# Fetching K and V of a decode-attention kernel in 4 MB transfers of 32 KB runs, eight heads interleaved, instead of 1 MB transfers of 8 KB runs

## The chip, the cores and the metric

The kernel runs on one core of one Trainium2 chip. The metric is the time of one execution on the device in microseconds (us). A run is in a *slow* state when it lies over 1.5% above the fastest of the same kernel; a single run of a kernel has the state *unknown*.

## The reference

One decode step: four batches, one new token each, attention over the last 2,048 of 8,192 cached positions, added to a small MLP.

```python
# x (4,1,576); k_cache, v_cache (4,16,8192,128) bf16; wq (576,4096); wo (4096,576)
xn = layernorm(x)
q  = (xn @ wq) -> (4, 32 heads, 1, 128)
k  = k_cache[:, :, 8192-2048:, :]         # each of 16 heads serves two q heads
v  = v_cache[:, :, 8192-2048:, :]
p  = softmax(q k^T * 128**-0.5)           # (4,32,1,2048)
attention = (p v) @ wo
mlp = x1 + gelu(layernorm(x1) @ w3) @ w4  # x1 = xn + gelu(layernorm(xn) @ w1), shifted, @ w2
out = x + attention + mlp
```

K and V in the window are 4 x 16 x 2048 x 128 x 2 bytes each, 67.1 MB together. The profile counts 88.5 MB read in all.

## The kernel before

Every transfer of K, V and the weights comes from one queue, in the order in which the program lists it. K comes into a ring of 7 slots and V into a ring of 9, each slot 1 MB. One unit of K or V is one head of two batches. Its source is written as 64 outer rows, each with 2 runs of 8 KB; together they fill 128 partitions.

```python
NKU, NVU, NT = 7, 9, 32
UE = NT * 128                               # 4096 bf16 = 8 KB in each partition

def kv_pairs(ring_t, slot, cache, u):
    g, pr = u // 2, u % 2
    return [(ring_t[:, slot * UE:(slot + 1) * UE],
             cache[pr:B:2, g, Sk - W:Sk, :].rearrange("b (i t) d -> i b (t d)", t=NT))]   # i 64, b 2

for u in range(NU):                         # NU = 32 units of K ...
    ev_k.append(add_dma(kv_pairs(kring_t, u % NKU, A_k_cache, u), ("k", u % NKU),
                        [f"T{4 * (u - NKU) + 3}"] if u >= NKU else [], u))
for u in range(NU):                         # ... then 32 of V, wo, w1, w2 among them
    ...
    ev_v.append(add_dma(kv_pairs(vring_t, u % NVU, A_v_cache, u), ("v", u % NVU), w, kk))
```

TensorE turns each 128x128 piece of K (`T{n}`), VectorE and ScalarE copy the turned piece out (`E{n}`), and products with a padded q give the scores (`SC`). After the last K, ScalarE takes the exponential, 32 transposes turn P, and products of V with P follow V as it lands. At the end w3 comes, then w4 in five pieces, whose 72 products (36 rows of 128, two halves of the columns) finish the sum:

```python
AO_CH = ((0, 4), (4, 7), (7, 8))            # the products with wo, in three pieces
W4P = [(0, 3, 0), (3, 6, 2), (6, 8, 4)]     # w4: pieces of 12, 12, 8, then 3 and 1 rows of 128
...
if n < last_p:
    add("pe", f, waits=[ev_w4[n], "gelu2"], sig=f"MO{n}", key=KT + 20 + n)
```

Of the kernel before, what the change touches and what calls it, by code (L numbers as in the profile page):

```python
# [12 lines left out]
NKU = 7  # L13
NVU = 9
# [5 lines left out]
WO_AFTER = 9  # L20
W12_AFTER = 11
AO_CH = ((0, 4), (4, 7), (7, 8))
# [13 lines left out]

def bass_parallel_sum__sliding_block_cached__mixer_s_mlp__decode_kernel(
# [8 lines left out]
    G = Hkv  # L46
    NU = 2 * G
    NT = 32
    UE = NT * 128
    NHB = 4 * NU  # L50
# [4 lines left out]
    HCH = [(0, 128), (128, 128), (288, 128), (416, 128), (256, 32), (544, 32)]  # L55
    x2 = A_x.rearrange("b s d -> (b s) d")
    o2 = out.rearrange("b s d -> (b s) d")

    with ExitStack() as ctx:
# [5 lines left out]

        kring_t = sb("kring", [128, NKU * UE], BF16)
        vring_t = sb("vring", [128, NVU * UE], BF16)
        W3E = 4 * F + FH
        regB_t = sb("regB", [128, max(NKT * 1024, W3E)], BF16)
        kring = kring_t[:].rearrange("p (s t d) -> p s t d", s=NKU, t=NT)  # L70
        vring = vring_t[:].rearrange("p (s t d) -> p s t d", s=NVU, t=NT)
        ktbuf = regB_t[:, 0:NKT * 1024].rearrange("p (s t d) -> p s t d", s=NKT, t=8)
        w3main = regB_t[:, 0:4 * F].rearrange("p (r n) -> p r n", r=4)
        w3rag = regB_t[:, 4 * F:W3E]
        wqmain = vring_t[:, 0:4 * Hq * Dh].rearrange("p (r n) -> p r n", r=4)
        wqrag = vring_t[:, 4 * Hq * Dh:4 * Hq * Dh + Hq * Dh // 2]
        WQ_SLOTS = -(-(4 * Hq * Dh + Hq * Dh // 2) // UE)
        wo_sb = kring_t[:, 0:Hq * D].rearrange("p (h r n) -> p h r n", h=8, r=4)
        _o = Hq * D
        w1main = kring_t[:, _o:_o + 4 * D].rearrange("p (r n) -> p r n", r=4)  # L80
        _o += 4 * D
        w1rag = kring_t[:, _o:_o + HALF]
        _o += HALF
        w2main = kring_t[:, _o:_o + 4 * D].rearrange("p (r n) -> p r n", r=4)
        _o += 4 * D
        w2rag = kring_t[:, _o:_o + HALF]
        _o += HALF
        assert _o <= NKU * UE
# [17 lines left out]
        Qpad_t = sb("Qpad", [128, 130 * G], BF16)  # L106
        Qpad = Qpad_t[:, 0:128 * G].rearrange("p (g b c) -> p g b c", g=G, b=B)
        ident_bf = sb("ident_bf", [128, 128], BF16)
        ident_f = sb("ident_f", [128, 128], FP32)
        ones_f = sb("ones_f", [128, 128], FP32)  # L110
        diag = sb("diag", [128, 128], FP32)
# [7 lines left out]
        P_sb = sb("P_sb", [128, NT, 64, 2], BF16)  # L119
        PT = sb("PT", [128, NT, 128], BF16)  # L120
# [3 lines left out]
        out_sb = sb("out_sb", [B, D], BF16)  # L124
# [4 lines left out]
        PTps = [ps[:, 4 + k, :].bitcast(BF16).rearrange("p (t r) -> p t r", t=8) for k in range(4)]  # L129
# [3 lines left out]
        OTbank = {g: 6 - n for n, (a, z) in enumerate(AO_CH) for g in range(2 * a, 2 * z)}  # L133
        OTps = lambda g: ps[:, OTbank[g], 0:128]
# [28 lines left out]
        def rag_src(w_ap):  # L163
            return w_ap[512:576, :].rearrange("r (h n) -> (r h) n", h=2)

        KS = float(NHB + 4)
        KV = KS + 4.0
        KT = KV + NU + 8.0


        P = lambda *a, **k: add("pool", *a, **k)
        P(lambda e: e.memset(zeros_bf[:], 0.0), sig="zeros_bf", key=-100)
        P(lambda e: e.memset(ident_bf[:], 1.0), sig="ib1", key=-99)
        P(lambda e: e.affine_select(out=ident_bf[:], in_=ident_bf[:], compare_op=ALU.is_equal, fill=0.0, base=0,
                                    pattern=[[-1, 128]], channel_multiplier=1), waits=["ib1"], sig="ident_bf", key=-98)
        P(lambda e: e.memset(ragsrc[:], 0.0), sig="rag_zero", key=-97)
        P(lambda e: e.memset(Qpad_t[:], 0.0), sig="qpad_zero", key=-96)
        P(lambda e: e.memset(P_sb[:], 0.0), sig="p_zero", key=-95)
        P(lambda e: e.memset(ident_f[:], 1.0), sig="if1", key=-94)
        P(lambda e: e.affine_select(out=ident_f[:], in_=ident_f[:], compare_op=ALU.is_equal, fill=0.0, base=0,  # L180
                                    pattern=[[-1, 128]], channel_multiplier=1), waits=["if1"], sig="ident_f", key=-93)
# [3 lines left out]

        ev_x = add_dma([(x_sb[:], x2)], "x", (), -100, engine="act")
        ev_wq, ev_k, ev_v, ev_w4 = [], [], [], []
        wq_src = A_wq[0:512, :].rearrange("(p r) n -> p r n", r=4)
        for r in range(4):
            ev_wq.append(add_dma([(wqmain[:, r, :], wq_src[:, r, :])], ("wq", r), (), -20 + r))  # L190
        ev_wq.append(add_dma([(wqrag, rag_src(A_wq))], ("wq", 4), (), -15))

        def kv_pairs(ring_t, slot, cache, u):
            g, pr = u // 2, u % 2
            return [(ring_t[:, slot * UE:(slot + 1) * UE],
                     cache[pr:B:2, g, Sk - W:Sk, :].rearrange("b (i t) d -> i b (t d)", t=NT))]

        def last_unit(nslots, s_lo, s_hi):
            return max(u for u in range(NU) if s_lo <= u % nslots <= s_hi)

        for u in range(NU):
            ev_k.append(add_dma(kv_pairs(kring_t, u % NKU, A_k_cache, u), ("k", u % NKU),
                                [f"T{4 * (u - NKU) + 3}"] if u >= NKU else [], u))
        wo_wait = f"T{4 * last_unit(NKU, 0, (_o - 1) // UE) + 3}"
        for u in range(NU):
            kk = KS + 0.01 * u
            w = [f"PV{u - NVU}"] if u >= NVU else (["q"] if u < WQ_SLOTS else [])
            ev_v.append(add_dma(kv_pairs(vring_t, u % NVU, A_v_cache, u), ("v", u % NVU), w, kk))
            if u == WO_AFTER - 1:
                wo_d = wo_sb.rearrange("p h r n -> p h (r n)")  # L210
                wo_s = A_wo.rearrange("(h p r) n -> p h (r n)", h=8, r=4)
                wo_8 = A_wo.rearrange("(h a p r) n -> h a p (r n)", h=8, a=8, r=4)
                ev_wo = add_dma([(wo_d[:, 0:6, :], wo_s[:, 0:6, :])] + [(wo_d[:, h, :], wo_8[h]) for h in (6, 7)],
                                "wo", [wo_wait], kk + 0.005)
            if u == W12_AFTER - 1:
                ev_w1 = add_dma([(w1main, B_w1[0:512, :].rearrange("(p r) n -> p r n", r=4)), (w1rag, rag_src(B_w1))], "w1",
                                [wo_wait], kk + 0.005)
                ev_w2 = add_dma([(w2main, B_w2[0:512, :].rearrange("(p r) n -> p r n", r=4)), (w2rag, rag_src(B_w2))], "w2",
                                [wo_wait], kk + 0.006)
        w3_src = B_w3[0:512, :].rearrange("(p r) n -> p r n", r=4)  # L220
        ev_w3 = [add_dma([(w3main[:, r, :], w3_src[:, r, :])], ("w3", r), [f"SC{G - 1}"], KT + r) for r in range(4)]
        ev_w3.append(add_dma([(w3rag, rag_src(B_w3))], ("w3", 4), [f"SC{G - 1}"], KT + 4))
        w4_main = B_w4[0:4096, :].rearrange("(c p r) n -> p c (r n)", p=128, r=4)
        w4_t3 = B_w4[4096:4480, :].rearrange("(p r) n -> p (r n)", r=3)
        w4_t1 = B_w4[4480:4608, :]
        w4tile = {}
        ev_w4 = []
        s4 = (NU - NVU) % NVU
        assert all((s4 + s_) % NVU + 2 <= NVU for s_ in (0, 2, 4))
        W4P = [(0, 3, 0), (3, 6, 2), (6, 8, 4)]  # L230
        for n, (c0, c1, s_) in enumerate(W4P):
            o0 = (s4 + s_) % NVU * UE
            v = vring_t[:, o0:o0 + (c1 - c0) * 4 * D].rearrange("p (c rn) -> p c rn", c=c1 - c0)
            ev_w4.append(add_dma([(v, w4_main[:, c0:c1, :])], ("w4", n), [f"PV{NU - NVU + s_ + 1}"], KT + 5 + n))
            for c in range(c0, c1):
                for q in range(4):
                    w4tile[4 * c + q] = v[:, c - c0, q * D:(q + 1) * D]
        o0 = (s4 + 4) % NVU * UE + 2 * 4 * D
        assert 2 * 4 * D + 4 * D <= 2 * UE
        v3 = vring_t[:, o0:o0 + 3 * D]  # L240
        v1 = vring_t[:, o0 + 3 * D:o0 + 4 * D]
        wl = [f"PV{NU - NVU + 5}"]
        ev_w4.append(add_dma([(v3, w4_t3)], ("w4", 3), wl, KT + 8))
        ev_w4.append(add_dma([(v1, w4_t1)], ("w4", 4), wl, KT + 9))
        for q in range(3):
            w4tile[32 + q] = v3[:, q * D:(q + 1) * D]
        w4tile[35] = v1
        W4N = [(12 * n, 12 * n + 12) for n in range(2)] + [(24, 32), (32, 35), (35, 36)]
        ev_o = [None, None]
        for h, eng in ((0, "sp"), (1, "act")):  # L250
            ev_o[h] = add_dma([(o2[:, HALF * h:HALF * (h + 1)], out_sb[:, HALF * h:HALF * (h + 1)])], ("out", h),
                              [f"fin{h}"], 10000, engine=eng)
            add(eng, lambda e: None, [ev_o[h]], None, 10001)
# [47 lines left out]
        for r in range(5):  # L301
            add("pe", pe_q(r), waits=[ev_wq[r], "xnT"], sig="q" if r == 4 else f"q_{r}", key=-30 + r)
# [310 lines left out]
```

## Time and profile before

| | before |
|---|---|
| time, median of 3 runs | 224.78 us (224.45 to 224.97) |
| span of the profiled run | 223.5 us |
| bytes read | 88.5 MB, of them K and V 67.1 MB |
| rate in 60 to 160 us | 418 GB/s |
| packet of 8,192 bytes | 312 ns (median of the packet records) |
| busiest engine | TensorE, 73% |

The first view is the page's span cut into 40 equal slices, of the kernel before. TensorE's and DMA's rows are busy tenths, PEclk is the clock granted to TensorE in tenths, GB/s is what the DMA engines moved.

```profile
PE   0469999999999999997257731666974436977596
...
PEclk9999999999999999999855555555695555875579
DMA  6999999999999999999999999999999999999940
GB/s 250 424 421 421 418 422 421 418 425 416 416 424 418 418 424 419 422 416 419 419 417 407 415 411 418 419 422 419 419 419 418 421 419 421 422 413 408 411 177 1
```

From the second to the 38th slice the DMA row stands at 9 and the rate at 407 to 425 GB/s. TensorE is nearly full as well up to the 18th slice, where K is turned, but the DMA row has no gap there, so its queue is not held up. Later TensorE has time to spare. The DMA bounds this kernel: 88.5 MB at 418 GB/s is 212 us of a span of 223.5.

The stretches of the end, of the kernel before (the window and its length, each engine's busy us with the instruction count in brackets, then granted clock, DMA share, GB/s; PE is TensorE, PEld its weight loads, DVE VectorE, ACT ScalarE, POOL GpSimd):

```profile
core 0: us, PE busy (x) PEld busy (x) DVE busy (x) ACT busy (x) POOL busy (x), PEclk, DMA share, GB/s
...
204.00:208.00 4.00, 2.59 (x70) 2.39 (x67) 0.00 (x0) 0.29 (x1) 0.00 (x0) 0.50 1.02 408
208.00:212.00 4.00, 2.59 (x11) 1.36 (x12) 0.00 (x0) 0.00 (x0) 0.00 (x0) 0.50 1.02 412
212.00:216.00 4.00, 4.00 (x21) 2.23 (x20) 0.00 (x0) 0.00 (x0) 0.00 (x0) 0.58 0.60 236
216.00:220.00 4.00, 4.00 (x35) 2.80 (x33) 0.00 (x0) 0.00 (x0) 0.00 (x0) 1.00 0.12 45
220.00:223.50 3.50, 1.30 (x11) 0.68 (x8) 0.45 (x1) 0.40 (x1) 0.00 (x0) 1.00 0.01 1
```

From 212 us the DMA is only partly busy, yet TensorE still works to 221. The next two lines are groups of the page for the kernel before: line, engine, operation, tiles, shapes and count; then busy us and the mean ns of one; then the idle time just before them and its releaser.

```profile
L324 PE MATMUL ps<-ident_bf,kring 128*128 128x128 bf16 x1024 | 67.2, 222 | 0.4 <-ACT regB L330 0.2
...
L426 PE MATMUL ps<-vring,h2T_sb 128*4 128x288 bf16 x72 | 11.9, 340 | 2.7 <-DMA vring<-in_B_w_dram 2.7
```

K's transposes (L324) have only 0.4 us of idle time before them: K is always there when TensorE is ready. The timeline has w4's 72 products begin at 209.41 us, when w4's first piece lands, and take 11.89 us.

### The profile page before, as it was taken

How to read it: one execution, taken by the hardware profiler on the slowest of the kernel's cores; microseconds unless marked ns; L12 is line 12 of the kernel's file. 1: busy time of each engine (PE TensorE's matmuls, PEld its weight loads, DVE VectorE, ACT ScalarE, POOL GpSimd, SP SyncE). 2: the span in 40 equal slices, each digit the busy share in tenths (PEclk: the TensorE clock that was granted, in tenths of full speed). 3: DMA queues.
4: the chain of work that ended last, by engine and by line, in shares of the span. 5: the costliest groups of instructions: out<-in, count | busy, mean ns of one | idle time of the engine just before them, and what ended most of it. 6: DMA issues, size and time to landing. Idle time of an engine off the chain costs nothing.

```text
span 223.5 us, 6245 instructions
## 1 busy us (share of the span) xinstructions
PE 162.7 (73%) x2934; PEld 124.7 (56%) x2934; DVE 70.9 (32%) x124; ACT 62.1 (28%) x76; POOL 7.9 (4%) x14
## 2 busy tenths in 40 slices
PE   0469999999999999997257731666974436977596
PEld 0457777777777777775047631544564335666263
DVE  5803565666666556664440000051000000000000
ACT  2001555555555555555594000001100000000000
POOL 8500000000000000000000000000000000000000
PEclk9999999999999999999855555555695555875579
DMA  6999999999999999999999999999999999999940
GB/s 250 424 421 421 418 422 421 418 425 416 416 424 418 418 424 419 422 416 419 419 417 407 415 411 418 419 422 419 419 419 418 421 419 421 422 413 408 411 177 1
DMA packets 13714, 88.91 MB, mean 398 GB/s; under 512 B 1388, under 2 KB 1784, under 8 KB 4472
## 3 DMA queue, kind: packets, MB, share of 16 engines
q1 hardware_dynamic: 13672, 88.50, 95.9%
q8 instruction: 23, 0.38, 0.7%
q14 instruction: 3, 0.02, 0.0%
q10 hardware_dynamic: 16, 0.01, 0.0%
HBM read 88.49 MB, written 0.00 MB: 396 GB/s over the span
## 4 chain that ended last, share of the span: by engine, by line
PE 47%; DMA 34%; ACT 12%; SPq 2%; issue 2%; DVE 1%
PE ps L324 23%; DMA vring<-in_A_v_cache_dram 15%; DMA vring<-in_B_w_dram 14%; PE ps L426 9%; ACT regB L330 8%; PE ps L340 8%; DMA vring<-in_A_wq_dram 5%; PE ps L405 5%; ACT P_sb L366 3%; SPq L159 2%; PE ps L312 1%; DVE rmax L360 1%; PE ps L375 0%; ACT PT L382 0%; PE ps L297 0%
## 5 line engine op out<-in xcount | busy, mean ns | idle before, releaser
L324 PE MATMUL ps<-ident_bf,kring 128*128 128x128 bf16 x1024 | 67.2, 222 | 0.4 <-ACT regB L330 0.2
L324 PEld LDWEIGHTS ps<-ident_bf,kring 128*128 128x128 bf16 x1024 | 58.5, 99 | 13.9 <-issue 7.3
L331 DVE COPY regB<-ps 128x1024 bf16<-128x1024 bf16 x80 | 52.3, 687 | 36.4 <-PE ps L324 34.6
L330 ACT ACTIVATE regB<-ps 128x1024 bf16<-128x1024 bf16 x48 | 47.5, 1022 | 48.4 <-PE ps L324 48.4
L405 PE MATMUL ps<-PT,vring 128*128 128x4 bf16 x1024 | 30.8, 166 | 29.9 <-DMA vring<-in_A_v_cache_dram 27.1
L405 PEld LDWEIGHTS ps<-PT,vring 128*128 128x128 bf16 x1024 | 29.0, 103 | 34.0 <-DMA vring<-in_A_v_cache_dram 28.8
L340 PE MATMUL ps<-regB,Qpad 128*32 128x512 bf16 x256 | 17.5, 392 | 4.5 <-ACT regB L330 4.5
L516 ACT ACTIVATE h2T_sb<-ps 128x144 bf16<-128x144 f32 x1 | 0.3, 291 | 49.6 <-PE ps L510 49.6
L426 PE MATMUL ps<-vring,h2T_sb 128*4 128x288 bf16 x72 | 11.9, 340 | 2.7 <-DMA vring<-in_B_w_dram 2.7
L440 DVE TENSOR_TENSOR OTn<-ps,rinvB 128x64 bf16<-128x64 f32 (+2 forms) x3 | 0.6, 202 | 38.5 <-PE ps L405 38.5
L340 PEld LDWEIGHTS ps<-regB,Qpad 128*32 128x32 bf16 x256 | 5.3, 94 | 11.1 <-ACT regB L330 5.9
L426 PE MATMUL ps<-kring,ORT 128*4 128x288 bf16 x64 | 11.0, 342 | 0.3 <-DVE ORT L444 0.3
L426 PEld LDWEIGHTS ps<-vring,h2T_sb 128*4 128x4 bf16 x72 | 7.1, 99 | 7.3 <-DMA vring<-in_B_w_dram 2.8
L262 ACT ACTIVATE sd<-mv 4x1 f32<-4x1 f32 x3 | 0.6, 202 | 35.0 <-DVE mv L260 35.0
L375 PE MATMUL ps<-ident_bf,P_sb 128*128 128x128 bf16 x32 | 4.1, 308 | 6.6 <-ACT P_sb L366 6.6
L531 DVE CAST out_sb<-ps 4x288 bf16<-4x288 f32 x1 | 0.4, 446 | 25.7 <-PE ps L426 25.7
L426 PEld LDWEIGHTS ps<-kring,ORT 128*4 128x4 bf16 x64 | 6.1, 99 | 4.4 <-DVE ORT L444 0.4
L478 DVE TENSOR_TENSOR x_bf<-ps,xn_bf 4x288 bf16<-4x288 f32 x2 | 0.9, 446 | 23.5 <-PE ps L473 23.5
L501 PE MATMUL ps<-x1nT,regB 128*128 128x4 bf16 x144 | 5.3, 172 | 3.0 <-DMA regB<-in_B_w_dram 2.9
L375 PEld LDWEIGHTS ps<-ident_bf,P_sb 128*128 128x128 bf16 x32 | 3.1, 138 | 7.9 <-ACT P_sb L366 7.9
L366 ACT ACTIVATE P_sb<-ps,negb 64x512 bf16<-64x512 f32 x8 | 6.6, 826 | 2.6 <-DVE negb L361 2.5
L276 PE MATMUL ps<-ident_bf,xn_bf 4*128 4x4 bf16 x8 | 0.5, 166 | 8.8 <-DVE ragsrc L269 8.4
(78 smaller groups left out, 69.7 us busy)
## 6 DMA issues: line engine op xcount, KB each, us to landing
kring<-in_A_k_cache_dram SPq DMA_DIRECT2D x32, 1024.0 KB, 12.1
vring<-in_A_v_cache_dram SPq DMA_DIRECT2D x32, 1024.0 KB, 21.2
regB<-in_B_w_dram SPq DMA_DIRECT2D x4, 1152.0 KB, 26.4
vring<-in_A_wq_dram SPq DMA_DIRECT2D x4, 1024.0 KB, 7.8
kring<-in_A_wo_dram SPq DMA_DIRECT2D x1, 3456.0 KB, 21.1
vring<-in_B_w_dram SPq DMA_DIRECT2D x2, 1728.0 KB, 30.9
kring<-in_A_wo_dram SPq DMA_DIRECT2D x2, 576.0 KB, 21.4
kring<-in_B_w_dram SPq DMA_DIRECT2D x2, 576.0 KB, 13.4
```

What stands on the lines that cost most here:

```text
L159: e.dma_start(o_, i_).then_inc(S[skey], 16)
L312: ins = e.matmul(ps[:, 4 + (w % NTB), :], lhsT=zeros_bf[:, 0:128], rhs=zeros_bf[:, :], start=True, stop=True)
L324: ins = e.transpose(tb[n % NTB][:, t, :], kring[:, u % NKU, 8 * k + t, :], ident_bf[:])
L330: return "act", lambda e: e.activation(out=ktbuf[:, n % NKT], in_=tb[n % NTB], func=ACTF.Copy)
L331: return "dve", lambda e: e.tensor_copy(out=ktbuf[:, n % NKT], in_=tb[n % NTB])
L340: ins = e.matmul(Sps[32 * b:32 * b + 32, c4, :].rearrange("p (t i) -> p t i", t=8), lhsT=Qpad[:, g, b, :], rhs=ktbuf[:, n % NKT, :, bh:128:2],
L360: add("dve", lambda e: e.tensor_reduce(out=rmax[:], in_=Sps, axis=AX.XY, op=ALU.max), waits=[f"SC{G - 1}"], sig="rmax", key=KS)
L366: add("act", lambda e, q=q, s=s, bh=bh: e.activation(out=P_sb[s, 8 * q:8 * q + 8, :, bh], in_=Sps[s, q, :].rearrange("p (t i) -> p t i", t ...
L375: ins = e.transpose(PTps[q][:, t, :], P_sb[:, 8 * q + t, :, :].rearrange("p i b -> p (i b)"), ident_bf[:])
L405: ins = e.matmul(o_, lhsT=vring[:, u % NVU, t, :], rhs=r_, start=(t == 0), stop=(t == NT - 1))
L426: return e.matmul(ACC[h], lhsT=lhsT, rhs=rhs, start=start, stop=stop)
L501: ins = e.matmul(H2Tps[:, n, :], lhsT=w3main[:, r, lo:hi:st], rhs=x1nT[:, r, :], start=(r == 0 and n == 0), stop=False, skip_group_check=True)
```

## The change

The intent is longer runs: 32 KB in each packet instead of 8 KB, so that fewer packets carry their fixed cost (9 ns each, by the line in the prediction that is fitted to the packets of the kernel before), in 4 MB transfers. One transfer holds eight heads of one batch. Its source has 16 outer rows, each with 8 runs of 32 KB, one for each head, so the partition of position block `i` and head `g` is `8i + g`. As heads are now mixed in the partitions, K's transposes use a permutation in place of the identity, P is multiplied with a mask for each head and turned by products, and P is padded with zeros for the products with V. K, V, wq, most of wo, w3 and w4 all go through one ring of five slots.

```diff
-NKU = 7
-NVU = 9
+NSLOT = 5
-WO_AFTER = 9
-W12_AFTER = 11
-AO_CH = ((0, 4), (4, 7), (7, 8))
+W4_ROWS = (18, 10, 5, 2, 1)
...
-    NT = 32
-    UE = NT * 128
+    NC = 8
+    NI = 16
+    NT = W // NI                 # 128
+    UE = NT * Dh                 # 32 KB in each partition
...
-        def kv_pairs(ring_t, slot, cache, u):
-            g, pr = u // 2, u % 2
-            return [(ring_t[:, slot * UE:(slot + 1) * UE],
-                     cache[pr:B:2, g, Sk - W:Sk, :].rearrange("b (i t) d -> i b (t d)", t=NT))]
+        def kv_src(cache, c):
+            b, gh = CH[c]
+            return cache[b, 8 * gh:8 * gh + 8, Sk - W:Sk, :].rearrange("g (i t) d -> i g (t d)", t=NT)
...
+        for c in range(1, NC):
+            w = ["q"] if c == 4 else ([f"T{NBLK * (c - NSLOT) + NBLK - 1}"] if c >= NSLOT else [])
+            ev_k[c, 0] = add_dma([(slot(k_slot(c)), kv_src(A_k_cache, c))], ("ring", k_slot(c)), w, c)
+        for c in range(NC):
+            w = [f"PV{c - 4}"] if c >= 4 else [f"T{NBLK * (c + 3) + NBLK - 1}"]
+            ev_v.append(add_dma([(slot(v_slot(c)), kv_src(A_v_cache, c))], ("ring", v_slot(c)), w, KS + c))
...    (wq in one transfer; wo on 128 rows throughout; w4 cut into 18, 10, 5, 2, 1 rows)
-                    ins = e.transpose(tb[n % NTB][:, t, :], kring[:, u % NKU, 8 * k + t, :], ident_bf[:])
+                    ins = e.transpose(tb[n % NTB][:, t, :], slot_t(k_slot(c))[:, 8 * k + t, :], perm_bf[:])
...
+            add("act", lambda e, q=q: e.activation(out=P_sb[:, q, :].rearrange("p (i t) -> p t i", t=32),
+                                                   in_=Sps[:, q, :].rearrange("p (t i) -> p t i", t=32), func=ACTF.Exp, ...
+                for u in range(8):
+                    ins = e.tensor_scalar(out=P8f[:, q % 2, u, :], in0=P_sb[:, q, :], scalar1=mask8[:, u // 4, u % 4:u % 4 + 1], ...
...
-                for t in range(8):
-                    ins = e.transpose(PTps[q][:, t, :], P_sb[:, 8 * q + t, :, :].rearrange("p i b -> p (i b)"), ident_bf[:])
+                for t in range(32):
+                    ins = e.matmul(PTps[q][:, t, :], lhsT=P8[:, q % 2, :, t],
+                                   rhs=sel_bf[:].rearrange("p c e -> p (c e)"), start=True, stop=True, skip_group_check=True)
...    (a second product and copy order P; padding of P; products with V and wo in the new order)
```

## The prediction

> **What bounds the kernel now.** The DMA. The page's 40 slices show all 16 DMA engines at 0.9 or more from the second slice to the 38th, at 416 to 424 GB/s; TensorE, the busiest engine, is at 73%. Buffers never starve the queue: it has no idle slice. So 88.5 MB at about 418 GB/s is 211 us, plus a start of 2 us and a tail. In the trace's packet records an 8,192-byte packet takes 312 ns, 9,216 bytes 349, 4,608 bytes 181, 1,152 bytes 51: about 9 ns plus 0.0369 ns per byte. A 4-byte completion packet costs 9 ns more per engine and transfer.[...]
>
> The tail: from 212 us half of the engines are done (stretches: DMA share 0.91, then 0.48 to 216 us). I put that to two 576 KB pieces of wo whose source has 8 rows[...]. The first w4 piece lands at 209.4 us; then 72 products take 11.9 us, 6 of them at half clock, and output ends at 223.5.
>
> **What changes, costed.**
> - K and V, 67.1 MB: packets of 32 KB instead of 8 KB. Estimate from the fit: 1,218 ns instead of 4 x 312; per engine 160.3 to 156.0 us. Gain 4.3 us, on the critical path.
> - wq in 32 KB rows: 0.2 us. w4 in rows of 20.7, 11.5, 5.8, 2.3, 1.2 KB: 0.5 us.
> - [...]
> - Together the last DMA lands about 6 us earlier, near 211 us instead of 217.
> - w4 now starts with half of its bytes in one piece, so the first lands about 6.4 us before the end: near 205.5. The 72 products still follow (11 to 12 us, beginning at half clock), so only about 4 us of the 6 reach the end.
> - Off the critical path: q products start after all of wq (first transposes about 21 us instead of 18.8); K is released in 4 MB steps; 128 small products against 32 transposes for P; 32 masks and 32 pads on VectorE. After V7 lands, 128 PV products and 32 wo products (before: 64 and 8 at the end) run; I estimate 18 us to the start of w4's products, just hidden by w3 and the first w4.
>
> **New wait.** One ring of five slots: after V3 (queue reaches its end about 130 us) w1, w2 and wo wait for the turned P. I estimate that between 125 and 131 us (scores end 111, max 2.3, exp 0.9 to 1.1 each, masks 0.2 to 0.35 each x 32, products at half clock). A stall of 0 to 5 us, mean 1, which would go straight into the time.
>
> **Predicted: 220.3 us, 217.3 to 223.6 (8 in 10).** Faster by over 2%: 0.48; within 2%: 0.46; slower: 0.06.
>
> **What would show it right.** K and V slices at 429 to 431 GB/s with packets of 32,768 bytes near 1.22 us; DMA share falling to zero within 2 us; first w4 landing near 205; products of w4 taking 11 to 12 us. Wrong: slices still near 419 (no gain from long runs, or rows 2 MB apart slowing reads); a hole in DMA at 128 to 136 us (P turned too late) or near 90 to 120 us (K slots freed too late).
>
> **What would make it wrong.** P's masks or strided weight loads slower than estimated (+5 us); TensorE late after V7, so that w4's products start after their data (+2); those products starting at full clock (-2.5).

Cut from this text is what no trace or run here shows, and with it a term that rested on it alone: 1 to 1.5 us for wo, whose last two pieces I took for the cause of the lag of half of the engines. That was my supposition, and e11_before_wo16 below refutes it. The terms left are 4.3, 0.2 and 0.5 us, together 5.0; with the one that is cut they came to 6.0 to 6.5, the "about 6 us" of the text. The 220.3 us are 4.5 us less than the 224.78 measured before; how they follow from 4 us that reach the end and a stall of 1 us in the mean, the text does not say.

## More of the kernel before

The page's list of transfers (count, size of each, us from issue to landing):

```profile
kring<-in_A_k_cache_dram SPq DMA_DIRECT2D x32, 1024.0 KB, 12.1
vring<-in_A_v_cache_dram SPq DMA_DIRECT2D x32, 1024.0 KB, 21.2
```

## The result, and the profile after

The changed kernel takes 387.94 us, the median of 5 fast runs (386.77 to 390.92); the kernel before took 224.67 us in the same rounds (224.34 to 224.97). The ratio is 1.731, with a 95% interval of 1.724 to 1.738. Ratios here and below are taken over fast runs, so they are not quite the ratios of the medians that I quote. The profile below is of the slowest of the five runs (390.92 us).

The same rows of the 40 slices, now of the changed kernel (a slice is 9.7 us, before it was 5.6):

```profile
PE   0555329292929292848367303051005630304997
...
PEclk9988859786867777688855555555555855555859
DMA  8999999999999999999999999999999999999950
GB/s 327 310 216 226 212 212 211 208 216 207 202 214 212 211 214 217 212 208 212 217 216 214 211 214 212 190 381 323 208 209 209 207 212 217 212 201 377 426 235 0
```

The DMA row is as full as before, but the rate is half: 201 to 217 GB/s in most slices. It rises to 310 to 426 in the slices in which the weights pass, and those come to 128 partitions as 128 outer rows. The DMA share doesn't fall when packets are slow, because it counts the time that packets take and not what they carry. The stretches of the middle show this in numbers, first of the kernel before:

```profile
core 0: us, PE busy (x) PEld busy (x) DVE busy (x) ACT busy (x) POOL busy (x), PEclk, DMA share, GB/s
60.00:110.00 50.00, 44.21 (x682) 32.98 (x680) 30.40 (x45) 27.23 (x28) 0.00 (x0) 1.00 1.01 419
110.00:160.00 50.00, 29.27 (x684) 23.39 (x685) 7.00 (x20) 10.78 (x22) 0.00 (x0) 0.50 1.02 417
```

and then of the changed kernel:

```profile
60.00:110.00 50.00, 32.20 (x441) 24.03 (x437) 19.26 (x29) 17.20 (x17) 0.00 (x0) 0.83 1.01 213
110.00:160.00 50.00, 29.05 (x350) 21.92 (x351) 14.33 (x21) 13.17 (x13) 0.00 (x0) 0.71 0.99 210
```

The share is 1.01 and 0.99 in both stretches of the changed kernel, and the rates are 213 and 210 GB/s against 419 and 417. The packet records (the start, duration and size of each packet, in the packed trace) tell the same: from 14 us on, where K and V pass, a packet of 32 KB takes a median of 2,504 ns. The 128 packets of wq are also of 32 KB, and took a median of 1,213 ns. Fewer engines are not the reason: the share is 1.01 and 0.99 of 16 engines, and in the packed trace of either kernel each transfer of K and V reports 16 completions, while x's transfer, of 4 rows, reports 5.

The groups and transfers of the page that answer to those shown before, and the exponentials:

```profile
L337 PE MATMUL ps<-perm_bf,ring 128*128 128x128 bf16 x1024 | 79.4, 245 | 66.8 <-DMA ring<-in_A_k_cache_dram 66.8
...
L444 PE MATMUL ps<-regB,ring 128*128 128x16 bf16 x1024 | 28.7, 174 | 107.2 <-DMA ring<-in_A_v_cache_dram 105.8
...
L385 ACT ACTIVATE Qpad<-ps,negb 128x512 bf16<-128x512 f32 x4 | 9.2, 2660 | 2.0 <-DVE negb L382 2.0
...
L473 PE MATMUL ps<-ring,h2T_sb 128*4 128x288 bf16 x72 | 11.1, 326 | 0.5 <-ACT h2T_sb L553 0.5
...
ring<-in_A_v_cache_dram SPq DMA_DIRECT2D x8, 4096.0 KB, 86.2
ring<-in_A_k_cache_dram SPq DMA_DIRECT2D x7, 4096.0 KB, 88.7
```

TensorE now waits 66.8 us in K's transposes and 107.2 us in V's products, nearly all of it for the K and V transfers. A piece of the chain of waits of the changed kernel shows the rhythm (start, us, what):

```profile
67.82 7.74 another core or an unknown queue
75.61 1.89 PE ps L337 x16
78.47 2.60 PE ps L337 x32
82.65 1.03 ACT regB L343
84.34 1.96 PE ps L337 x32
87.89 7.58 another core or an unknown queue
95.52 1.89 PE ps L337 x16
```

Each 4 MB of K costs one period: the transposes of one transfer begin at 75.61, those of the next at 95.52. That is 19.9 us for 4.19 MB, or 211 GB/s. The pieces named an unknown queue are the waits for those transfers; the group of L337 above names them.

So the time went into the rate of K and V. 67.1 MB at 212 GB/s is 316 us, and at before's 418 GB/s 160 us. The difference of 156 us is nearly all of the 163 us lost.

### The profile page after: what moved, and what is told of

Same layout as the page of the kernel before. It is cut to its first block, busy times and chain, and to the rows that moved or that the text cites. A ratio compares the mean times of both kernels' runs of the same rounds, so it can differ in the third digit from the quotient of the medians.

```text
span 389.2 us, 6411 instructions
## 1 busy us (share of the span) xinstructions
PE 185.1 (48%) x3014; PEld 143.5 (37%) x3014; DVE 88.1 (23%) x194; ACT 68.8 (18%) x75; POOL 5.3 (1%) x17
## 4 chain that ended last, share of the span: by engine, by line
PE 36%; another core or an unknown queue 25%; DMA 19%; SPq 12%; ACT 5%; DVE 1%; issue 1%
PE ps L337 17%; SPq L170 12%; DMA ring<-in_A_v_cache_dram 11%; DMA ring<-in_A_k_cache_dram 9%; PE ps L473 6%; PE ps L356 5%; PE ps L444 4%; ACT Qpad L385 2%; ACT regB L343 2%; PE ps L543 2%; PE ps L403 1%; DVE rmax L381 1%; PE ps L547 1%; PE ps L414 0%
## 5 line engine op out<-in xcount | busy, mean ns | idle before, releaser
L337 PE MATMUL ps<-perm_bf,ring 128*128 128x128 bf16 x1024 | 79.4, 245 | 66.8 <-DMA ring<-in_A_k_cache_dram 66.8
L337 PEld LDWEIGHTS ps<-perm_bf,ring 128*128 128x128 bf16 x1024 | 70.6, 111 | 86.6 <-DMA ring<-in_A_k_cache_dram 69.1
L444 PE MATMUL ps<-regB,ring 128*128 128x16 bf16 x1024 | 28.7, 174 | 107.2 <-DMA ring<-in_A_v_cache_dram 105.8
L444 PEld LDWEIGHTS ps<-regB,ring 128*128 128x128 bf16 x1024 | 28.2, 104 | 108.9 <-issue 73.6
L433 DVE TENSOR_TENSOR regB<-PT,mU_bf 128x512 bf16<-128x512 bf16 x32 | 11.3, 418 | 44.3 <-PE ps L444 41.6
L403 PE MATMUL ps<-sel_bf,regB 128*128 128x16 bf16 x128 | 8.5, 208 | 7.4 <-DVE regB L394 7.3
L473 PE MATMUL ps<-ring,h2T_sb 128*4 128x288 bf16 x72 | 11.1, 326 | 0.5 <-ACT h2T_sb L553 0.5
L473 PE MATMUL ps<-ring,ORT 128*4 128x288 bf16 x56 | 10.5, 365 | 0.5 <-DVE ORT L492 0.3
L385 ACT ACTIVATE Qpad<-ps,negb 128x512 bf16<-128x512 f32 x4 | 9.2, 2660 | 2.0 <-DVE negb L382 2.0
L394 DVE TENSOR_SCALAR regB<-Qpad,mask 128x512 bf16<-128x512 bf16 x32 | 8.8, 348 | 2.7 <-ACT Qpad L385 2.6
```

The source lines that it names most:

```text
L337: ins = e.transpose(tb[n % NTB][:, t, :], slot_t(k_slot(c))[:, 8 * k + t, :], perm_bf[:])
L385: add("act", lambda e, q=q: e.activation(out=P_sb[:, q, :].rearrange("p (i t) -> p t i", t=32), in_=Sps[:, q, :].rearrange("p (t i) -> p t ...
L394: ins = e.tensor_scalar(out=P8f[:, q % 2, u, :], in0=P_sb[:, q, :], scalar1=mask8[:, u // 4, u % 4:u % 4 + 1], scalar2=None, op0=ALU.mult)
L403: ins = e.matmul(PTps[q][:, t, :], lhsT=P8[:, q % 2, :, t], rhs=sel_bf[:].rearrange("p c e -> p (c e)"), start=True, stop=True, skip_group ...
L433: return lambda e: e.tensor_tensor(out=PTpad[:, c % 2, ts_], in0=PTv[:, ts_, cc, :].unsqueeze(2).to_broadcast([128, 32, 8, 2]), in1=mU_bf[ ...
L444: ins = e.matmul(o_, lhsT=slot_t(v_slot(c))[:, t, :], rhs=PTpad[:, c % 2, t].rearrange("p u e -> p (u e)"), start=(t == 0), stop=(t == NT ...
```

## The experiments

Three theories were open after the result.

- **Destination.** How the transfer is cut over the partitions that it writes decides the rate. This was my supposition. No trace records which engine writes which partition, so only the rates of runs with other destinations could test it.
- **Source.** Rows of heads lie 2 MB apart in HBM, and reading them in step is slow.
- **Packets.** Packets of 32 KB are slow in themselves. wq's 1,213 ns spoke against it from the start.

The texts written before the runs call these theories PORT, HBM and SIZE. The numbers that PORT expected are my estimates, set against measured packets (wq's 1,213 ns, the changed kernel's 2,504 ns, later e1_flat's 1,222 and e4_perhead's 4,079 ns).

Some kernels below read wrong rows of K and V, or put them in wrong partitions. With these inputs the attention's part of the output is so small that the comparison on the chip passes them too. So I also compared those that should be right in simulation, on inputs scaled up until attention matters: the changed kernel, e6, e7, e8, e9, e11 and e12 gave an rms error of 0.0038 against an attention part of 0.53, and the wrong ones 0.67 to 0.78.

### e1_flat: the same bytes as 128 outer rows (wrong values)

```diff
-            return cache[b, 8 * gh:8 * gh + 8, Sk - W:Sk, :].rearrange("g (i t) d -> i g (t d)", t=NT)
+            flat = cache.rearrange("b g s d -> (b g s d)")
+            return flat[c * 128 * UE:(c + 1) * 128 * UE].rearrange("(p x) -> p x", p=128)
```

> The changed kernel, but every 4 MB of K and V is one contiguous run of memory, 128 rows of 32 KB (the values are wrong on purpose). Theory PORT[...] and theory HBM[...]: both expect 32 KB packets of about 1215 ns, 430 GB/s, and a time near my first forecast, 218 to 223 us. Theory SIZE (32 KB packets or 4 MB transfers are slow in themselves, or the queue is starved by the coarser ring): still 2500 ns and about 388 us.

Measured: 225.96 us, median of 3 fast runs (224.59 to 226.33; a fourth, slow run took 228.58), ratio 1.004 (0.999 to 1.009). Packets of 32 KB took a mean of 1,222 ns, and 427 GB/s passed in 60 to 110 us. All of the rest of the change was in this kernel, so the loss of 163 us, but for about 1 us, lies in how K and V are addressed. Packets of 32 KB are not slow in themselves. The time missed my 218 to 223, though. One reason is in these stretches of e1_flat:

```profile
126.00:130.00 4.00, 3.75 (x50) 3.01 (x50) 1.36 (x6) 1.81 (x4) 0.00 (x0) 0.50 0.95 410
130.00:134.00 4.00, 4.00 (x130) 3.77 (x131) 2.11 (x7) 2.24 (x3) 0.00 (x0) 0.50 0.72 258
134.00:140.00 6.00, 4.79 (x161) 4.63 (x161) 3.06 (x9) 0.00 (x0) 0.00 (x0) 0.50 0.96 345
140.00:144.00 4.00, 3.06 (x114) 3.06 (x115) 0.26 (x1) 0.00 (x0) 0.00 (x0) 0.50 1.02 419
```

From 130 to 140 us the DMA moved 258 and 345 GB/s. At 410 GB/s the same ten microseconds would have carried 1.0 MB more, which is 2.4 us. This is the hole that I had feared: w1, w2 and wo wait until P is turned. The exponentials took 2.48 to 2.72 us each, where I had estimated 0.9 to 1.1.

### e2_addr and e3_heads64: the source

e2_addr keeps 16 outer rows with 8 runs and moves the source rows to a pitch of 36 KB, the heads to 2 MB and 10 KB (wrong values). e3_heads64 keeps rows 2 MB apart and takes 64 heads with 2 runs of 32 KB in each (wrong values).

```diff
e2_addr:
+            LG, LI = Sk * Dh + 5120, UE + 2048
+            rows = flat[c * 7 * Sk * Dh:c * 7 * Sk * Dh + 8 * LG].rearrange("(g l) -> g l", g=8)
+            return rows[:, 0:NI * LI].rearrange("g (i x) -> i g x", i=NI)[:, :, 0:UE]
e3_heads64:
+            rows = cache.rearrange("b g s d -> (b g) s d")
+            s0 = Sk - W + 256 * c
+            return rows[:, s0:s0 + 256, :].rearrange("g (i t) d -> g i (t d)", t=NT)
```

> The changed kernel, with the transfer's form kept (16 outer rows by 8 inner, the same partitions), but with the source rows 36 KB apart instead of 32 KB and the eight groups 2 MB + 10 KB apart instead of 2 MB (values wrong on purpose). HBM expects the powers of two to be the cause, so 1215 ns packets and about 220 us. PORT expects no change: about 2500 ns a packet, 212 GB/s, 388 us.

> The changed kernel, with each 4 MB taken as 64 heads by 2 runs of 32 KB (every row is read once over the kernel, but into other places, so values are wrong on purpose). The source's outer count is 64, as in the kernel before, and its rows lie 2 MB apart. PORT expects 1215 ns packets, 430 GB/s, about 220 us. HBM expects no gain or worse[...]: 2500 ns or more, 388 us or more.

Measured: e2_addr took 386.77 us, its packets a mean of 2,476 ns in 60 to 160 us (the changed kernel 2,483): moving the rows changed next to nothing. e3_heads64 took 229.11 us, its packets a mean of 1,231 ns after 40 us, but 1,374 from 13 to 40 us, where e1_flat has 1,216; these 13% I leave open. Its rows are 2 MB apart and it is fast; e2_addr's are not and it is slow. As the cause of the factor of two, the theory of the source falls.

### e4_perhead and e9_perhead8: eight transfers, two destinations

Both cut each 4 MB transfer into eight, one for a head, with 16 rows each. e4_perhead writes a head into 16 neighbouring partitions (wrong values). e9_perhead8 writes it where the changed kernel has it, into every eighth partition (right values).

```diff
e4_perhead (cut):
+  add_dma([(slot(k_slot(c))[16 * g:16 * g + 16], kv_src(A_k_cache, c)[:, g]) for g in range(8)], ...
e9_perhead8 (calls cut):
+        def per_head(tile, rows):
+            return [(tile[g:128:8], rows[:, g]) for g in range(8)]
```

> The changed kernel, with each 4 MB split into eight transfers of one head each, 16 rows of 32 KB into 16 neighbouring partitions. [...]only the partitions written differ (values wrong on purpose). PORT: [...]about half of the changed kernel's rate: 5000 ns a packet, 106 GB/s, 650 to 720 us. HBM: as the changed kernel, 2500 ns and 388 us.

> As e4_perhead (eight transfers of one head, 16 rows of 32 KB each[...]), but row i of head g is written to partition 8i+g, as in the changed kernel, so the values are right. From e4_perhead only the destination partitions differ. PORT: [...]2500 ns a packet, 212 GB/s, 385 to 395 us. If the number of transfers or their 16-row source set the rate and not the partitions: as e4_perhead, about 4000 ns and 558 us.

Measured: e4_perhead took 557.67 us, with a mean of 4,079 ns for a packet and 128 GB/s in 60 to 160 us. The direction was right, the size not: I had expected 5,000 ns and 106 GB/s. e9_perhead8 took 388.79 us, with 2,468 ns and 213 GB/s in the same stretch. The two have the same source rows, the same sizes and the same count of transfers; only the destination partitions differ, and with them the rate, by 1.7. e9_perhead8 also agrees with the changed kernel. Neither comes to the full rate, though: these two show that the partitions count, not that they are all that the changed kernel's form costs.

### e5_before_16x8: the suspected form in the kernel before (wrong values)

```diff
-            g, pr = u // 2, u % 2
+            b, gh, w0 = u // 8, u // 4 % 2, Sk - W + 512 * (u % 4)
-                     cache[pr:B:2, g, Sk - W:Sk, :].rearrange("b (i t) d -> i b (t d)", t=NT))]
+                     cache[b, 8 * gh:8 * gh + 8, w0:w0 + 512, :].rearrange("g (i t) d -> i g (t d)", t=NT))]
```

> The kernel before, with one thing altered: each 1 MB transfer of K and V takes 16 runs of eight heads instead of 64 runs of two batches, so the source has 16 outer rows of eight (all rows are read once, into other places: values wrong on purpose). Packets stay at 8 KB, transfers at 1 MB, the rings as they were. PORT: packets of about 620 ns instead of 312, 212 GB/s in K and V, about 375 to 390 us. A theory that needs the 32 KB runs or the 4 MB transfers for the slowness: 312 ns, 225 us.

Measured: 354.20 us. Transfers were 1 MB and runs 8 KB as before, and only the split into 16 outer rows of 8 instead of 64 of 2, with the rows that follow from it, was new. In 60 to 160 us a packet of 8 KB took a mean of 558 ns instead of 314, and 237 GB/s passed. So the loss comes with this split, with packets of 8 KB as with those of 32 KB. It was a factor of 1.8 here, less than the 2 that I had expected; why the smaller packets lose a little less is open.

### e6_fix, e7_fix_exp, e8_fix_tail: kernels with right values

e6_fix splits a batch into four heads with 32 outer rows: 2 MB transfers with runs of 16 KB, ten slots. e7_fix_exp is e6_fix with an exponential that writes in order, leaving the reordering to the masks. e8_fix_tail is e7_fix_exp with the products of wo in three pieces again and w4 in eight pieces.

```diff
e6_fix against the changed kernel (masks, permutations and indices follow; cut):
-NSLOT = 5
+NSLOT = 10
-    NC = 8
-    NI = 16
+    NC = 16
+    NI = 32
-    CH = [(b, gh) for gh in range(2) for b in range(B)]
+    CH = [(b, g) for g in range(4) for b in range(B)]
e7_fix_exp against e6_fix:
-            add("act", lambda e, q=q: e.activation(out=P_sb[:, q, :].rearrange("p (i t) -> p t i", t=16),
-                                                   in_=Sps[:, q, :].rearrange("p (t i) -> p t i", t=16), func=ACTF.Exp,
+            add("act", lambda e, q=q: e.activation(out=P_sb[:, q, :],
+                                                   in_=Sps[:, q, :], func=ACTF.Exp,
e8_fix_tail against e7_fix_exp (cut):
-W4_ROWS = (18, 10, 5, 2, 1)
+W4_ROWS = (6, 6, 6, 6, 6, 3, 2, 1)
+        AO_CH = ((0, 2), (2, 3), (3, 4))
```

> The changed kernel with each chunk made of four heads by 32 runs of 16 KB (2 MB, ten slots) instead of eight heads by 16 runs of 32 KB; masks, permutations and pads follow, and values are right. The source has 32 outer rows, four to each[...]. PORT: 16 KB packets of 611 to 615 ns, about 427 GB/s, 222 to 227 us (as the contiguous run, whose other costs it shares). If 32 outer rows are split like 16: 1230 ns and about 388 us.

> e6_fix, with the exponentials written in the order they are read (contiguous); the masking on VectorE does the reordering in its place. In the changed kernel and in the contiguous run each exponential of 128x512 took 2.3 to 2.7 us with writes 64 bytes apart. I expect about 0.7 us each here, P turned 5 to 7 us earlier, the hole of some 3 us in the DMA near 130 us gone, and 2 to 3 us less than e6_fix. If that hole is not on the critical path: no difference.

> e7_fix_exp, with the attention's last product in three pieces (16 products after the last V instead of 32) and w4 in rows of 6, 6, 6, 6, 6, 3, 2, 1 instead of 18, 10, 5, 2, 1, so that w3's weight loads step by 12 bytes instead of 36 and w4's products start with a sixth of the data. I expect w4's products to begin about 5 us earlier and the end 3 to 5 us earlier than e7_fix_exp: 216 to 220 us, faster than the kernel before by 2 to 4%.

Measured, against 224.91 us of the kernel before in the same rounds:

| | median us | ratio (95%) | K and V packets | GB/s in 60 to 110 us |
|---|---|---|---|---|
| e6_fix | 225.51 | 1.005 (1.001 to 1.008) | 16 KB, 613 ns | 426 |
| e7_fix_exp | 225.00 | 1.000 (0.996 to 1.003) | as e6_fix | 425 |
| e8_fix_tail | 220.42 | 0.981 (0.978 to 0.983) | as e6_fix | 424 |

With 32 outer rows of 4 the rate is whole again, and a packet of 16 KB takes a median of 613 ns, which is what the line fitted to the packets of the kernel before gives (614). Yet e6_fix is not faster than the kernel before: the 7 GB/s won (426 against 419) don't reach the end.

e7_fix_exp answers to the theory that the exponentials are to blame. The groups of the exponentials, first of e6_fix, then of e7_fix_exp:

```profile
L379 ACT ACTIVATE Qpad<-ps,negb 128x512 bf16<-128x512 f32 x4 | 9.0, 2622 | 2.0 <-DVE negb L376 2.0
```

```profile
L379 ACT ACTIVATE Qpad<-ps,negb 128x512 bf16<-128x512 f32 x4 | 2.7, 685 | 2.0 <-DVE negb L376 2.0
```

One exponential fell from 2,622 to 685 ns by writing in order. The time did not change (225.51 against 225.00, intervals that overlap), where I had expected 2 to 3 us. e6_fix had no such hole in its DMA as e1_flat: 403 GB/s in 134 to 140 us. A faster exponential was off the path there.

e8_fix_tail took 4.6 us off e7_fix_exp. Its stretches at the end answer to those of the kernel before:

```profile
200.00:204.00 4.00, 4.00 (x97) 4.00 (x95) 0.00 (x0) 0.00 (x0) 0.00 (x0) 0.50 1.01 411
204.00:208.00 4.00, 3.53 (x33) 2.23 (x32) 0.00 (x0) 0.29 (x1) 0.00 (x0) 0.50 1.01 419
208.00:212.00 4.00, 3.94 (x32) 2.50 (x31) 0.00 (x0) 0.00 (x0) 0.00 (x0) 0.99 0.79 314
212.00:216.00 4.00, 3.70 (x31) 2.38 (x29) 0.00 (x0) 0.00 (x0) 0.00 (x0) 1.00 0.31 123
216.00:220.00 4.00, 0.30 (x3) 0.00 (x0) 0.45 (x1) 0.40 (x1) 0.00 (x0) 0.79 0.01 1
```

w4's products begin at 205.3 us instead of 209.07 in e7_fix_exp and 209.41 in the kernel before, and TensorE is at full clock from 208 us. In the kernel before it was so only from about 215 us. This is the fastest version, 2.0% faster than the kernel before (the interval straddles the 2% line, so it is unclear whether it is over 2%; that it is faster is clear).

### e12_before_w4 and e11_before_wo16: parts of the tail in the kernel before

e12_before_w4 is the kernel before with w4 cut as in e8_fix_tail. e11_before_wo16 is the kernel before with the two pieces of wo that had 8 outer rows written as 128 rows.

```diff
e12_before_w4 (cut):
+        for n, rc in enumerate((6, 6, 6, 6, 6, 3, 2, 1)):
+            ev_w4.append(add_dma([(v, B_w4[base:base + 128 * rc, :].rearrange("(p r) n -> p (r n)", r=rc))], ("w4", n),
+                                 [f"PV{NU - NVU + n}"], KT + 5 + n))
e11_before_wo16:
-                ev_wo = add_dma([(wo_d[:, 0:6, :], wo_s[:, 0:6, :])] + [(wo_d[:, h, :], wo_8[h]) for h in (6, 7)],
+                ev_wo = add_dma([(wo_d[:, 0:6, :], wo_s[:, 0:6, :])] + [(wo_d[:, h, :], wo_s[:, h, :]) for h in (6, 7)],
```

> The kernel before, with w4 alone brought in rows of 6, 6, 6, 6, 6, 3, 2, 1 as in e8_fix_tail. If the gain of e8_fix_tail over e7_fix_exp (4.6 us) lies in the order of the tail and not in K and V, w4's products begin near 207 us instead of 209.4 and end by the landing of the last piece: 1.5 to 2.5 us less than the kernel before. If the faster K and V are needed for it: no gain.

> The kernel before, with its last two pieces of wo (576 KB each) read as 128 rows like the others instead of 8 by 128. My prediction said that these two [...]make half of the engines late by 4 us at the end, and that without them the end comes 1 to 1.5 us earlier. Rival, from the completion times of e6_fix and e8_fix_tail, which have no such piece and show the same 4 us between the two halves: the lag has another source, and the time stays within 0.5 us or grows.

Measured: e12_before_w4 took 222.69 us (222.65 to 222.77), ratio 0.991 (0.989 to 0.993), w4's products from 207.33 us. So about 2 of e8_fix_tail's 4.5 us need nothing of the new K and V form. How the other 2.5 us are shared between the longer packets and the order of wo's products I did not separate. e11_before_wo16 took 224.06 us, ratio 0.998 (0.995 to 1.001). My prediction put the lag of half of the engines at the end down to those two pieces and expected 1 to 1.5 us. That is refuted, though not by a changed program: the two programs were the same byte for byte. So their times differ by noise alone, and the 8 outer rows stood only in the Python text. The trace agrees: in both kernels wo's three transfers report 48 completions, 16 for each, as many as each transfer of K and V, so these pieces were on all 16 engines from the start. With them so, the 16 completions of the last piece of w4 still come in two groups of eight, 212.89 to 213.99 and 216.07 to 218.15 us (in the trace of the kernel before 212.66 to 213.94 and 216.20 to 217.86).

### e13 to e16: the destination alone

These four start from e1_flat, with its contiguous rows, and cut each 4 MB into parts (wrong values). e13, e14 and e15 write parts of 64, 32 and 16 rows into as many neighbouring partitions. e16 writes the same 64 rows as e13 into every second partition.

```diff
+        def in_parts(tile, rows):
e13_flat64:
+            return [(tile[64 * j:64 * j + 64], rows[64 * j:64 * j + 64]) for j in range(2)]
e14_flat32:
+            return [(tile[32 * j:32 * j + 32], rows[32 * j:32 * j + 32]) for j in range(4)]
e15_flat16:
+            return [(tile[16 * j:16 * j + 16], rows[16 * j:16 * j + 16]) for j in range(8)]
e16_flat64s2:
+            return [(tile[j:128:2], rows[64 * j:64 * j + 64]) for j in range(2)]
```

> e1_flat (contiguous 4 MB, 430 GB/s with 128 rows), each 4 MB in two transfers of 64 rows of 32 KB, into partitions 0 to 63 and 64 to 127 (values wrong on purpose). PORT: [...]about 2450 ns a packet, 212 GB/s, 380 to 390 us. If only a source of 16 outer rows is slow: 1215 ns, 226 us.

> e1_flat in four transfers of 32 rows into 32 neighbouring partitions each (wrong on purpose). PORT: [...]as e13_flat64: 2450 ns, 212 GB/s, 380 to 390 us. If the count of rows sets the rate: clearly slower than e13_flat64. If only 16 outer rows are slow: 226 us.

> e1_flat in eight transfers of 16 rows into 16 neighbouring partitions each (wrong on purpose). From e4_perhead only the source addresses differ (contiguous instead of heads 2 MB apart). PORT: [...]as e4_perhead: 3800 to 4200 ns, about 136 GB/s, 540 to 570 us. If e4_perhead owed part of its slowness to its source: faster than 540 us.

> e13_flat64 with only the destination altered: the 64 rows go to every second partition, first the even ones and then the odd ones[...] (wrong on purpose). PORT: faster than e13_flat64, up to 1215 ns and 226 us[...]; as e13_flat64[...]. A count of rows: as e13_flat64.

| | partitions of one transfer | us | 32 KB packet, mean ns in 60 to 110 us | GB/s in 60 to 110 us |
|---|---|---|---|---|
| e1_flat | 128 | 225.96 | 1,222 | 427 |
| e13_flat64 | 64, neighbouring | 390.74 | 2,510 | 211 |
| e14_flat32 | 32, neighbouring | 390.20 | 2,508 | 210 |
| e15_flat16 | 16, neighbouring | 587.27 | 4,330 | 124 |
| e16_flat64s2 | 64, every second | 226.00 | 1,221 | 428 |

The stretches of e13_flat64, then of e16_flat64s2:

```profile
60.00:110.00 50.00, 32.08 (x442) 23.94 (x439) 19.30 (x29) 17.22 (x17) 0.00 (x0) 0.80 1.01 211
```

```profile
60.00:110.00 50.00, 48.61 (x763) 36.29 (x761) 32.21 (x48) 28.09 (x28) 0.00 (x0) 1.00 1.00 428
```

These two kernels differ in one thing, the partitions that a transfer of 64 contiguous rows writes. Neighbouring ones give 211 GB/s, every second one 428, at the same DMA share. So for transfers of 64 rows the destination alone makes the factor of two. For the changed kernel's own form, 16 outer rows of 8 in one transfer, the same cause is argued from this and from e4_perhead and e9_perhead8, and not shown: no run with 16 rows in a transfer came to the full rate, whatever it wrote to. The text on e16_flat64s2 had left both outcomes open, a rate up to e1_flat's and one as e13_flat64's. 64 and 32 neighbouring partitions are equally slow, with 211 and 210 GB/s. 16 of them are slower still: e15_flat16 shows 124. I had expected 136 there, and 540 to 570 us.

### e10_perhead7: another spread of the partitions (wrong values)

```diff
+        def per_head(tile, rows):
+            return [(tile[g:g + 106:7] if g < 7 else tile[112:128], rows[:, g]) for g in range(8)]
```

> As e9_perhead8, but heads 0 to 6 go to partitions 7i+g and head 7 to partitions 112 to 127 (values wrong on purpose). [...]PORT: most packets between 1215 and 1700 ns, 300 to 400 GB/s in K and V, 235 to 290 us. If a source of 16 outer rows is slow whatever it is written to: 2500 ns or more, 385 us or more.

Measured: 371.55 us, where I had expected 235 to 290 us. Packets took a median of 2,194 ns (1,653 to 3,004 without the lowest and the highest tenth), and 222 GB/s passed in 60 to 160 us, where I had expected 300 to 400. A step of 7 partitions gained only 4% on the step of 8 (e9_perhead8, 388.79 us), each a single run. The slices of e10_perhead7 show two speeds in turn:

```profile
GB/s 341 337 248 234 259 184 257 194 252 186 246 195 244 202 250 183 266 186 256 175 269 197 268 200 268 153 400 322 241 206 245 218 229 220 222 187 369 430 280 1
```

Rates near 250 and near 190 GB/s alternate. Why they do, and why the mean is so low, no run shows.

## Why the prediction was wrong, point by point

- **What bounds the kernel** was right. The DMA did, and the change acted on the DMA.
- **The failed step** is "K and V, 67.1 MB: packets of 32 KB instead of 8 KB. Estimate from the fit: 1,218 ns instead of 4 x 312", with its gain of 4.3 us. The fit itself was good: wq's packets took 1,213 ns, e1_flat's 1,222, and e6_fix's of 16 KB 613. But it is a function of the packet's size alone, taken from transfers of the kernel before, which moved 418 GB/s in 60 to 160 us. In the changed kernel a packet of K or V took 2,504 ns, so that K and V took about 316 us (67.1 MB at 212 GB/s) in place of the 156.0 that I had put down. What the step left out is the form of the transfer: 16 outer rows with 8 runs each. The runs showed that this form costs a factor of two (e1_flat against the changed kernel), nearly that at 8 KB too (e5_before_16x8), and that in transfers of 16 or 64 rows the partitions written change the rate (e4_perhead against e9_perhead8, e13_flat64 against e16_flat64s2). I had asked no more of K and V than their packets' size. All 16 engines were busy all the time (a DMA share of 1.00 in 60 to 160 us, and 16 completions for each transfer), at half the rate (212 GB/s against 418).
- **"Rows 2 MB apart slowing reads"**, the risk that I named for a slow rate, was not the cause (packets of 2,476 ns in e2_addr with the rows moved, where the changed kernel has 2,483, and of 1,231 ns after 40 us in e3_heads64 with rows 2 MB apart).
- **The lag of half of the engines** I put to wo's pieces. They ran on 16 engines in the kernel before as well (48 completions for three transfers), so the 1 to 1.5 us that I booked for them were never to be had. The lag's source is open.
- **The exponentials** I estimated at 0.9 to 1.1 us each; they took 2.48 to 2.72, because they write with a stride (2.62 us with a stride in e6_fix, 0.69 in order in e7_fix_exp). The masks, estimated at 0.2 to 0.35 us, took 0.348. In the kernel before, an exponential of 64x512 took 0.83 us and a copy of 128x1024 on VectorE 0.69. In e1_flat, where the DMA ran at full rate, the predicted stall for P appeared, about 2.4 us instead of a mean of 1. In the changed kernel it doesn't matter beside the rate.
- **The tail.** I estimated 18 us from V7's landing to the start of w4's products; it was 20.9 us (355.0 to 375.85). I had the last DMA land 6 us earlier. With K and V at full rate it landed at 215.95 us (e1_flat) and 215.19 (e7_fix_exp) against 217.86, which is 1.9 to 2.7 us earlier. My 4 us of gain at the tail assumed w4's first piece, of 18 rows, at 205.5 and its products following at once. In e1_flat it landed at 209.72 and they began at 211.15; in e7_fix_exp at 208.94 and 209.07. So it was mostly this large piece that came too late; TensorE, with the whole second half of wo's products after V7, added 1.4 us in e1_flat and 0.1 in e7_fix_exp. e8_fix_tail shows that the gain is to be had: smaller pieces (the first landed at 204.76), and wo in three.
- **With the DMA's rate mended**, the rest of the change was worth nothing by itself: e6_fix 1.005 and e7_fix_exp 1.000 times the time before.

What stays open: which engine writes which partition in the form with 16 outer rows, as the trace doesn't record it; whether a transfer with 16 outer rows can come to the full rate at all; why e10_perhead7 gained only 4%; why packets into 16 neighbouring partitions took 3.3 to 3.5 times as long as e1_flat's (4,079 and 4,330 ns against 1,222), where those into 64 or 32 took 2.1 times (2,510 and 2,508); why packets of 8 KB lost 1.8 times and not 2.

## What to carry to other kernels

When a transfer's access pattern changes, cost it by the partitions that its rows reach and by how many outer rows it is cut into, not only by its bytes and its run length. Here 64 rows to neighbouring partitions moved 211 GB/s and to every second one 428 (e13_flat64, e16_flat64s2); a source of 64 outer rows with 2 runs in each moved 419 (the kernel before), 32 with 4 moved 426 (e6_fix) and 16 with 8 moved 213 (the changed kernel), all in 60 to 110 us. A DMA share of 1.00 says nothing of the rate (1.01 at 419 and at 213 GB/s): set the duration of one packet against its size, and against a packet of the same size that is known to be fast. Fast packets took 51 ns for 1,152 bytes, 159 for 4,096, 312 for 8,192, 613 for 16,384 and 1,213 for 32,768, close to 9 ns and 0.0369 ns for each byte. Longer packets won a few GB/s (426 against 419) that didn't reach the end (225.51 us against 224.91), while the order and size of the last pieces did (220.42 us in e8_fix_tail).
